# Turning the scaled keys on VectorE and through HBM, with the state's update one unit later, in a fused RWKV6 and SiLU kernel

## Chip, core and metric

The kernel runs on one core of one Trainium2 chip. The metric is the time of one execution on the device in microseconds (us): 628.24 us before the change, the median of three runs between 627.59 and 628.37. All tensors are fp32.

## What is computed

```python
# r, k, v, w: (4, 8, 768, 48), u: (8, 48)
for t in range(S):                                   # S = 768 tokens
    cur = einsum('bhd,bhe->bhde', u * k_t, v_t)
    y[:, :, t] = einsum('bhd,bhde->bhe', r_t, state + cur)
    state = w_t[:, :, :, None] * state + einsum('bhd,bhe->bhde', k_t, v_t)
x = y.transpose(0, 2, 1, 3).reshape(3072, 384)
h = x @ w_in                                         # 384 x 2048
out = (h / (1 + exp(-h))) @ w_out                    # 2048 x 384
```

The first half is a linear recurrence over tokens with a 48x48 state for each of 4 batches x 8 heads. The second half is a dense layer up, SiLU, and a dense layer down.

## The kernel before

**Units.** Tokens are cut into 6 chunks of 128, batches into 2 pairs. A unit is one chunk of one pair, so there are 12, numbered 0 to 11 here and in the code: the "fifth to tenth" units of the change are units 4 to 9. Units i and i + 2 are consecutive chunks of the same pair, so unit i + 2 is the next to read the state that unit i updates.

**Within a unit.** Keys are scaled by products of the decays w, queries likewise, in seven levels of doubling block size. Scores of a level are a small matmul (line 669), merged into the score tile by VectorE under a mask (`keep_masked`, line 679). When all levels are done, the tile `tk` holds keys scaled to the end of the chunk. Then `y_state` (line 794) multiplies queries by the old state, `y` (line 807) multiplies scores by values, and `update` (line 813) makes the new state: keys times values in PSUM tile `p_kv` (line 821), the old state decayed by GpSimd (line 826), their sum by VectorE (line 835).

**Turning the keys.** `tk` has the head dimension on partitions, and `update` wants tokens there. `turn_k` (line 773) turns it: eight TensorE transposes of 128x128 against an identity a unit (line 781), into PSUM, and two ScalarE copies to the tile `kq` (line 782).

**Turning the inputs.** `load_blocks` (line 100) loads w, r and k in 32-token blocks into `raw`, a buffer with two slots (unit i and unit i + 2 share one), in 16 small transfers for each of the three tensors and unit, all issued on SyncE's queue. `turn` (line 346) turns them on VectorE, two 32x32-block transposes for each tensor (line 360).

**The dense half** runs behind by one and two units. `up` (line 924) is 12 matmuls into one of two PSUM buffers `p_h` and one ScalarE SiLU out of it (line 938), so the third `up` can start only when the SiLU of the first has emptied its buffer. The down layer is done in seven block products, `quarter` (line 981), each 16 matmuls into one of two PSUM buffers `p_o` (line 995), emptied by ScalarE for the first (line 1002) and by VectorE for the rest (line 1004).

**Order.** The schedule is written out by hand: every engine does its instructions in the order in which the program lists them. `mix` (line 867) gives a unit as a list of groups. For units from 4 on there are eleven, 0 to 10; the main loop runs a group and then some steps of the dense half:

```python
room = (1, 1, 0, 2, 1, 1, 1, 1, 1, 2, 2, 1, 1, 0) if i < NPAIR else (3, 2, 2, 1, 1, 1, 2, 1, 1, 1, 0)
for group, count in zip(groups, room):
    do(*group)
    for step in steps[:count]:
        do(*step)
```

The steps are the seven quarters of unit i - 2 (after groups 0, 1 and 2) and the eight `up` of unit i - 1 (one after each of groups 3, 4 and 5, two after group 6, one after each of 7, 8 and 9). Group 3 holds the scores of levels 3 and 4 (`burst`), the move of the small block sums through HBM (`block_move`, line 537) and the large token loads of the next unit (`load_rk`, line 131). Group 5 prepares levels 5 and 6 (a ScalarE copy at line 595 and one at line 739). Group 6 spreads the block sums (ScalarE, lines 548 and 550; then VectorE, lines 551 and 557). Group 7 holds the scores of levels 5 and 6. Group 9 turns the keys and the next unit's inputs. Group 10 holds `y_state`, `y`, `update` and `move_x` (line 849), which brings y into the layout of the dense half in ten transfers.

**Loads.** The transfers of `load_blocks` for unit i + 2 are twelve list entries of four transfers each, w first, then k, then r, with `load_values` for unit i + 1 in the middle. They are spread over groups 1 to 10 (line 916), always at the end of a group, so ahead of the dense steps that follow the group.

Of the kernel before, what the change touches and what calls it, by code (L numbers as in the profile page):

```python
# [8 lines left out]
F32 = mybir.dt.float32  # L9
# [29 lines left out]
def kernel(  # L39
# [11 lines left out]
    nc = tc.nc  # L51
# [5 lines left out]
    NB = 2  # L57
    NP = H // 2
    PD = 64
    Q = NB * NP  # L60
# [5 lines left out]
    units = [(n, b0) for n in range(S // L) for b0 in range(0, B, NB)]  # L66
    NSLOT = 2
    NTOK = 2
    NPAIR = 4
# [4 lines left out]
    const = ctx.enter_context(tc.tile_pool(name="const", bufs=1))  # L74
    pin = ctx.enter_context(tc.tile_pool(name="pin", bufs=1))
    pt = ctx.enter_context(tc.tile_pool(name="pt", bufs=2))
# [4 lines left out]
    raw = const.tile([128, NSLOT, 3, NB, H, PD], F32, name="raw")  # L81
    WRK = {"w": 0, "r": 1, "k": 2}
# [17 lines left out]
    def load_blocks(i, name, g):  # L100


        n, b0 = units[i]
        src, t0 = {"w": w, "r": r, "k": k}[name], n * L + g * 32
        room = raw[:, i % NSLOT, WRK[name]].rearrange("p b h d -> p (b h d)").rearrange("p (q g d) -> p q g d", q=Q, d=32)
        for e in range(2):
            for a in range(2):
                d0, d1 = a * 32, min(D, a * 32 + 32)
                nc.sync.dma_start(out=room[(2 * e + a) * 32:(2 * e + a + 1) * 32, :, g, 0:d1 - d0],
                                  in_=src[b0:b0 + NB, e::2, t0:t0 + 32, d0:d1].rearrange("b q t d -> t (b q) d"))  # L110

    def load_values(i):
# [54 lines left out]
    scratch = ctx.enter_context(tc.tile_pool(name="scratch", bufs=2, space=bass.MemoryType.DRAM))  # L167
# [109 lines left out]
    room = pt.tile([128, 4, DM // 2], F32, name="partial", bufs=1).rearrange("p x d -> p (x d)")  # L277
# [66 lines left out]
    tw, tr, tk, diag, kq, xt = {}, {}, {}, {}, {}, {}  # L344
# [106 lines left out]
    at = 768  # L451
# [312 lines left out]
    def turn_apart(i):  # L764

        apart[i] = [ps.tile([128, NB, NP, D], F32, name="p_sc", bufs=2) for e in range(2)]
        for x in range(Q):
            for e, to in enumerate(apart[i]):
                rows = slice(PD * e, PD * e + D)
                nc.tensor.transpose(to[:, x // NP, x % NP], tk[i][rows, NP + (x if x < NP else NP + Q - 1 - x), :],  # L770
                                    ident[rows, rows])

    def turn_k(i, b):
        kq[i, b] = pt.tile([128, NP, 2 * PD], F32, name="kq")
        if i < NTOK:
            for e, have in enumerate(apart[i]):
                nc.scalar.copy(out=kq[i, b][:, :, PD * e:PD * e + D], in_=have[:, b])
            return
        p_tr = ps.tile([128, NP, 2 * PD], F32, name="p_m", bufs=2)
        for p in range(NP):  # L780
            nc.tensor.transpose(p_tr[:, p, :], tk[i][:, NP + (p, 2 * NP - 1 - p)[b], :], ident)  # L781
        nc.scalar.copy(out=kq[i, b], in_=p_tr)

    p_yt, p_kv, yt = {}, {}, {}

# [75 lines left out]
    def both(fn, i, *args):  # L861
        return [(fn, i, b, *args) for b in range(NB)]

    def block_loads(i):
        return [(load_blocks, i, name, g) for name in "wkr" for g in range(4)]

    def mix(i):

        ahead = i + 1 < len(units)

        def at(now, *steps):
            return steps if now else ()

        def bonus_steps(j, *steps):
            return [(block_bonus, j, x) for x in steps]

        def sum_steps(j, *steps):
            return [(block_sum, j, x) for x in steps]

        def turns(j):  # L880
            return [*both(turn, j, "w"), (product, j, 0), *both(turn, j, "k"), *both(turn, j, "r"), (grow_own, j, 0)]

        def start(j):
            return [*[(product, j, l) for l in range(1, NL)], (grow_own, j, 1)]

        end = [[*at(ahead, *bonus_steps(i + 1, 0, 1, 2, 3))],
               [*at(i < len(units) - NB, *both(turn_k, i)), *at(ahead, *turns(i + 1))],
               [*both(y_state, i), *both(y, i), *both(update, i), *at(ahead, *start(i + 1)),
                *at(ahead, *sum_steps(i + 1, 0, 1), *bonus_steps(i + 1, 4, 5)), (move_x, i)]]
        if i < NPAIR:  # L890
            groups = [[*both(turn, i, "w"), (product, i, 0)],
                      [*both(turn, i, "k"), *both(turn, i, "r"), (odd_ones, i)], [(start_levels, i), (prepare_keys, i, 1)],
                      [(prepare, i, 1), *[(product, i, l) for l in range(1, NL)]],
                      [(burst, i, 1), (keep_level, i, 1)],
                      [(keep_level, i, 2), (go_on, i, 2)],
                      [(prepare, i, 3), (reverse_v, i), (bonus, i, 0)],
                      [(burst, i, 3), (keep_level, i, 3), (bonus_sum, i, 0), (bonus, i, 1), (bonus, i, 2)],
                      [(keep_level, i, 4), (go_on, i, 4), (bonus_sum, i, 1), (load_rk, i + 1), (load_u,)],
                      [(prepare, i, 5), (make_block_mask,), (bonus_spread, i), (bonus_write, i)],
                      [(burst, i, 5), (keep_level, i, 5), (keep_level, i, 6), (go_on, i, 6)], *end]  # L900
        else:
            groups = [[], [(odd_keys, i, 2), (grow_keys, i, 2, False), (grow_queries, i, 2), *sum_steps(i, 2)],
                      [(prepare, i, 3), *bonus_steps(i, 6, 7)],
                      [(burst, i, 3), (keep_level, i, 3), *sum_steps(i, 3, 4), (block_move, i), *at(ahead, (load_rk, i + 1))],
                      [(keep_level, i, 4), (go_on, i, 4)],
                      [(prepare, i, 5), (reverse_v, i)],
                      [(block_spread, i), (block_write, i)],
                      [(burst, i, 5), (keep_level, i, 5), (keep_level, i, 6), (go_on, i, 6)], *end]

        loads = block_loads(i + NSLOT) if i + NSLOT < len(units) else []  # L910
        if i + 1 < len(units):
            loads.insert(len(loads) // 2, (load_values, i + 1))

        behind = groups[10 if i < NPAIR else 1:]
        for at, group in enumerate(behind):
            group += loads[at * len(loads) // len(behind):(at + 1) * len(loads) // len(behind)]
        return groups
# [114 lines left out]
    def back(fn, i, *args):  # L1032
# [6 lines left out]
       (make_dense,), (beat, 16))  # L1039

    blocks = block_loads(2)
    others = {1: [(clear, 0), (beat, 6)], 2: [(turn, 1, 0, "r"), (head_weight, 0), (beat, 2)],
              3: [(turn, 1, 1, "r"), (head_weight, 1), (beat, 2)], 4: [(turn, 1, 1, "w"), (reverse_v, 0)],
              5: [(bonus_spread, 0), (bonus_write, 0), (turn, 1, 0, "w")], 6: [*both(turn_in, 1, "k"), *blocks[0:4], (tail_weight, 0)]}
    for l in range(1, NL):
        do((scores, 0, l), *[(grow_keys, 0, l + 1)] * (l + 1 < NL), *others[l])

    do((bonus, 1, 0), (bonus, 1, 1), (bonus, 1, 2), *both(y, 0), (turn_apart, 0), (join_weight, 0), (add_weight,),
       (product, 1, 0), (tail_weight, 1), (turn, 1, 0, "k"), (join_weight, 1), (dense_x, 0, 0), (turn, 1, 1, "k"),
       (dense_x, 0, 1), (grow_queries, 1, 0), (odd_ones, 1), (tail_weight, 2), *both(turn_k, 0), (head_weight, 2),  # L1050
       (start_keys, 1, nc.gpsimd, True), (add_weight,), (up, 0, 0), (join_weight, 2), *blocks[4:8],
       (start_keys, 1, nc.gpsimd, False), (add_weight,), (tail_weight, 3), (odd_keys, 1, 1), (head_weight, 3), (grow_keys, 1, 1),
# [11 lines left out]
    for m in range(1, 4):  # L1064
# [3 lines left out]

    do((scores, 1, NL - 1), (join_weight, 8), (add_weight,), (up, 0, 7), *both(y, 1), (turn_apart, 1),
       (tail_weight, 9), *both(turn_k, 1), (dense_x, 1, 0), (head_weight, 9, [0]), (dense_x, 1, 1), (head_weight, 9, [1]),  # L1070
       (join_weight, 9), (add_weight,), (tail_weight, 10), (head_weight, 10), *both(update, 1), (up, 1, 0), *both(turn, 2, "w"))
    blocks = block_loads(3)

    others = {0: [(up, 1, 1), (down, 0, 0, 0), *both(turn, 2, "k"), (product, 2, 0), (product, 2, 1)],
# [20 lines left out]
    for i in range(3, len(units)):  # L1095
        steps = downs(i - 2) + ups(i - 1)
        groups = mix(i)
        if i == NTOK + 1:

            groups[2].append((weight_sums, 2))  # L1100
            groups[4].insert(1, (weight_sums, 3))
# [5 lines that stand above are left out]
            steps = steps[count:]  # L1107
# [32 lines left out]
```

## Time and profile before

| | |
|---|---|
| time, median of 3 | 628.24 us |
| span of the profiled execution | 626.6 us |
| TensorE matmul, share of span | 99% |
| VectorE | 70% |
| GpSimd | 58% |
| ScalarE | 30% |
| all transfers | 203067 packets, 53.25 MB, mean 85 GB/s |
| of these under 512 bytes | 186752 packets |

One unit in the middle of the kernel, from one burst of level 3 to the next, takes 48.74 or 48.75 us for units 4 to 9. Units 10 and 11 update no state and take 47.15 us.

How to read it: busy shares are averages over the whole span. The chain of waits is followed back from the last instruction to what released it; its shares say which engine and line the end hung on. A row of a timeline gives the start in us from the start of the span, how long it lasted, the engine (SPq is SyncE's queue), the line of the kernel, the tiles and the count; a bracket at its end is the idle time ahead of it and what ended that. A row of the groups ends with busy us and mean ns of one instruction, then the idle time ahead of them.

### The profile page before, as it was taken

The page shows a single profiled execution, that of the slowest core. Times are in us where ns is not written, and L with a number is a line of the kernel's source. Part 1 is how long each engine was busy: PE and PEld are TensorE (multiplying, and loading weights), DVE is VectorE, ACT ScalarE, POOL GpSimd, SP SyncE. Part 2 cuts the span into 40 slices and gives each one's busy share as a digit, 9 for nine tenths or more (in the row PEclk, how much of TensorE's full clock was granted, in tenths as well). Part 3 has the DMA queues.
Part 4 walks back from the last instruction along what each step waited for, and adds up shares of the span by engine and source line. Part 5 has one row for each costly group of instructions (what it writes and reads, how often), then busy time and mean ns, then how long its engine had stood idle before and what let it go on. Part 6 is the DMA issues. An engine that isn't in the chain of part 4 may idle for free.

```text
span 626.6 us, 12324 instructions
## 1 busy us (share of the span) xinstructions
PE 620.3 (99%) x4606; PEld 562.8 (90%) x4606; DVE 438.6 (70%) x749; ACT 187.4 (30%) x380; POOL 363.7 (58%) x414
## 2 busy tenths in 40 slices
PE   8999999999999999999999999999999999999997
PEld 8888876799899899899899899889889989989997
DVE  6879779898995694794794595686596596571041
ACT  6798882221321320320320321221221221220110
POOL 6998388566676567567577378378378458400000
PEclk9999999999999999999999999999999999999999
DMA  9966874443543643543543543542542312100000
GB/s 227 291 154 163 164 203 49 88 79 66 101 68 50 133 66 68 106 69 63 105 67 54 110 65 52 115 64 51 115 70 50 77 33 51 35 1 27 25 1 25
DMA packets 203067, 53.25 MB, mean 85 GB/s; under 512 B 186752, under 2 KB 194816, under 8 KB 203008
## 3 DMA queue, kind: packets, MB, share of 16 engines
q1 hardware_dynamic: 201424, 51.88, 41.1%
q10 hardware_dynamic: 1584, 0.59, 0.4%
q8 instruction: 36, 0.59, 0.4%
q14 instruction: 23, 0.19, 0.1%
HBM read 43.21 MB, written 5.24 MB: 77 GB/s over the span
## 4 chain that ended last, share of the span: by engine, by line
PE 94%; POOL 1%; DVE 1%; ACT 1%; DMA 1%; issue 1%; POOLq 0%; ACTq 0%
PE p_h L929 41%; PE p_o L995 32%; PE p_sc L669 5%; PE p_m L951 3%; PE p_m L807 3%; PE p_m L794 3%; PE p_m L669 3%; PE p_m L781 1%; PE p_sc L821 1%; DMA raw<-in_k_dram 1%; PE p_m L372 1%; POOL tk L625 1%; PE p_m L845 0%; DVE score L584 0%; POOL w_in_sb L241 0%
## 5 line engine op out<-in xcount | busy, mean ns | idle before, releaser
L929 PE MATMUL p_h<-xt,w_in_sb 128*128 128x256 f32 x1152 | 258.1, 382 | 0.7 <-POOL tk L649 0.7
L929 PEld LDWEIGHTS p_h<-xt,w_in_sb 128*128 128x128 f32 x1152 | 215.9, 190 | 32.6 <-POOL tk L649 0.9
L938 ACT ACTIVATE gt<-p_h 128x512 f32<-128x512 f32 x90 | 53.7, 597 | 256.1 <-PE p_h L929 255.9
L625 POOL TENSOR_TENSOR tk<-tk,tw 128x256 f32<-128x256 f32 x128 | 88.7, 714 | 62.4 <-ACT tk L595 34.7
L995 PE MATMUL p_o<-own,temps 128*128 128x192 f32 x528 | 87.9, 326 | 0.0
L995 PE MATMUL p_o<-w_out_sb,gt 128*128 128x192 f32 x508 | 87.3, 328 | 0.0
L995 PEld LDWEIGHTS p_o<-own,temps 128*128 128x128 f32 x528 | 86.0, 190 | 0.2
L995 PEld LDWEIGHTS p_o<-w_out_sb,gt 128*128 128x128 f32 x508 | 82.7, 190 | 0.9 <-issue 0.4
L487 POOL TENSOR_TENSOR ruk<-tokens_rk 128x768 f32<-128x768 f32 (+1 forms) x32 | 48.5, 1527 | 46.3 <-DMA tokens_rk<-in_k_dram 33.7
L977 DVE TENSOR_TENSOR temps<-gt 128x256 f32<-128x256 f32 x84 | 55.4, 660 | 18.3 <-ACT gt L938 18.3
L408 POOL TENSOR_TENSOR tw<-tw 128x256 f32<-128x256 f32 (+6 forms) x83 | 43.8, 528 | 40.2 <-DVE tw L360 36.3
L679 DVE COPY_PREDICATED score<-mask,p_sc 128x512 f32<-128x512 int8 x62 | 44.5, 772 | 13.4 <-PE p_sc L669 12.7
L607 DVE TENSOR_TENSOR tr<-tr,tw 128x512 f32<-128x512 f32 x61 | 49.6, 813 | 3.7 <-POOL tk L625 1.1
L595 ACT COPY tk<-tk 128x256 f32<-128x256 f32 x52 | 20.9, 403 | 85.4 <-POOL tk L625 67.1
L1004 DVE TENSOR_TENSOR partial<-p_o,partial 128x192 f32<-128x192 f32 x33 | 11.8, 358 | 47.2 <-PE p_o L995 47.1
L669 PEld LDWEIGHTS p_sc<-tr,tk 48*128 48x128 f32 x512 | 31.4, 187 | 10.3 <-issue 7.3
L669 PE MATMUL p_sc<-tr,tk 48*128 48x128 f32 x512 | 37.7, 285 | 0.7 <-POOL tk L625 0.6
L1004 DVE TENSOR_TENSOR temps<-p_o,partial 128x192 f32<-128x192 f32 x22 | 7.9, 358 | 33.3 <-PE p_o L995 23.1
L995 PE MATMUL p_o<-w_out_sb,temps 128*128 128x192 f32 x176 | 30.4, 326 | 0.0
L995 PEld LDWEIGHTS p_o<-w_out_sb,temps 128*128 128x128 f32 x176 | 28.9, 190 | 0.0
L487 POOL TENSOR_TENSOR tokens_rk<-tokens_rk,tokens_w 128x192 f32<-128x192 f32 (+1 forms) x32 | 26.8, 857 | 1.3
L977 DVE TENSOR_TENSOR temps<-temps,gt 128x256 f32<-128x256 f32 x43 | 25.7, 598 | 1.5
(170 smaller groups left out, 828.0 us busy)
## 6 DMA issues: line engine op xcount, KB each, us to landing
w_out_sb<-in_moe_w_in_dram SPq DMA_DIRECT2D x6, 768.0 KB, 7.0
w_out_sb<-in_moe_w_out_dram SPq DMA_DIRECT2D x4, 768.0 KB, 5.1
own<-in_moe_w_out_dram SPq DMA_DIRECT2D x4, 768.0 KB, 5.1
tokens_rk<-in_r_dram SPq DMA_DIRECT2D x8, 384.0 KB, 4.5
tokens_rk<-in_k_dram SPq DMA_DIRECT2D x8, 384.0 KB, 5.3
tokens_w<-in_w_dram SPq DMA_DIRECT2D x8, 384.0 KB, 6.6
xt<-yt SPq DMA_DIRECT2D x60, 48.0 KB, 2.0
raw<-in_w_dram SPq DMA_DIRECT2D x80, 32.0 KB, 2.3
```

The lines of the kernel that those rows point to most:

```text
L408: engine.tensor_tensor(out=up, in0=t[:, :, 0::2], in1=t[:, :, 1::2], op=ALU.mult)
L487: mul = lambda out, one, two: nc.gpsimd.tensor_tensor(out=out, in0=one, in1=two, op=ALU.mult)
L595: nc.scalar.copy(out=keys(i, X[(l + 1) % 2] * L + c, [4 * c, blocks], [c, 2], [1, c]), in_=keys(i, NP * L + c, [4 * c, blocks], [NP * L + ...
L607: nc.vector.tensor_tensor(out=odd, in0=odd, in1=tw[i][l][:, :, 0::2][:, :, :, None].to_broadcast([128, Q, L >> (l + 1), c]), op=ALU.mult)
L625: nc.gpsimd.tensor_tensor(out=out, in0=have, in1=odd_products(i, l, b, *blocks), op=ALU.mult)
L669: nc.tensor.matmul(bass.AP(tensor=s_p.tensor, offset=s_p.offset, ap=[s_p.ap[0], [apart * L // 2, 2], [1, L // 2]]), lhsT=tk[i][rows, X[l % ...
L679: nc.vector.copy_predicated(out=dst, mask=masks[l][:, :, None].to_broadcast([128, NB, NP, ni, c]), data=sc[e].rearrange("p (b q) (i c) -> ...
L929: nc.tensor.matmul(p_h[:, a, :], lhsT=w_in_sb[:, c, f * 128:(f + 1) * 128], rhs=xt[i][:, c, :], start=(c == 0), stop=(c == KC - 1))
L938: nc.scalar.activation(out=gt[i, m], in_=p_h, func=AF.Silu)
L977: nc.vector.tensor_tensor(out=out, in0=one, in1=two, op=op)
L995: nc.tensor.matmul(p, lhsT=left(f), rhs=right[:, f, :], start=(f == 0), stop=(f == FH - 1))
L1004: nc.vector.tensor_tensor(out=to, in0=p, in1=known, op=ALU.add)
```

## The change

For units 4 to 9 the keys are no longer turned on TensorE. VectorE turns the 32x32 blocks of `tk` into the room of the w slot in `raw` that it has just read (`turn_keys`), four transfers put the blocks in their places in a scratch tensor in HBM, and four more, early in the next unit, bring them into one tile for all keys (`load_keys`). That takes TensorE's transposes and ScalarE's copies away for these units. Since the keys come back only in the next unit, `update` of a unit runs in the next one, after its `y`; values are thus needed one unit longer, and the load of values, whose two buffers would otherwise be taken too early, moves to the start of their own unit. The block loads for units 6 to 11 come in the order k, r, w, since the w room is in use for longer, and those of r are issued on ScalarE's queue in place of SyncE's.

```diff
@@ load_blocks
-                nc.sync.dma_start(out=room[...], in_=src[...])
+                queue = nc.scalar if i > NPAIR + 1 and name == "r" else nc.sync
+                queue.dma_start(out=room[...], in_=src[...])
@@
+    all_keys = const.tile([128, Q, 2 * PD], F32, name="all_keys")
     def turn_k(i, b):
-        kq[i, b] = pt.tile([128, NP, 2 * PD], F32, name="kq")
+        kq[i, b] = all_keys[:, b * NP:(b + 1) * NP]
@@
+    def turn_keys(i):
+        room = raw[:, (i + 1) % NSLOT, WRK["w"]].rearrange("p b h d -> p (b h d)")
+        to = room.rearrange("p (g x d) -> p x g d", g=4, d=32)
+        for b in range(NB):
+            row0 = NP + b * NP
+            x = to[:, b * NP:(b + 1) * NP]
+            nc.vector.transpose(out=x[:, ::-1] if b == 1 else x, in_=tk[i][:, row0:row0 + NP, :].rearrange("p q (g d) -> p q g d", d=32))
+        turned_keys[i] = scratch.tile([32, Q * 4, 4, 32], F32, name="turned_keys")
+        for x in range(4):
+            nc.sync.dma_start(out=turned_keys[i][:, :, x], in_=room[x * 32:(x + 1) * 32].rearrange("t (y d) -> t y d", d=32))
+
+    def load_keys(i):
+        have = turned_keys.pop(i).rearrange("t (g q) x d -> t g q (x d)", g=4)
+        for b in range(NB):
+            kq[i, b] = all_keys[:, b * NP:(b + 1) * NP]
+        for g in range(4):
+            nc.sync.dma_start(out=all_keys[g * 32:(g + 1) * 32], in_=have[:, g])
@@ block_loads
-        return [(load_blocks, i, name, g) for name in "wkr" for g in range(4)]
+        return [(load_blocks, i, name, g) for name in ("wkr" if i < NPAIR + NSLOT else "krw") for g in range(4)]
@@ mix
-            return [*both(turn, j, "w"), (product, j, 0), ...]
+            return [*both(turn, j, "w"), *at(NPAIR <= j - 1 < len(units) - NB, (turn_keys, j - 1)), (product, j, 0), ...]
@@
+        ready = i if i < NPAIR else i - 1
-               [*at(i < len(units) - NB, *both(turn_k, i)), *at(ahead, *turns(i + 1))],
-               [*both(y_state, i), *both(y, i), *both(update, i), ...
+               [*at(i < NPAIR, *both(turn_k, i)), *at(ahead, *turns(i + 1))],
+               [*both(y_state, i), *both(y, i), *at(i != NPAIR and ready < len(units) - NB, *both(update, ready)), ...
@@
-            groups = [[], [(odd_keys, i, 2), ...
+            groups = [[*at(i > NPAIR, (load_values, i)), *at(NPAIR <= i - 1 < len(units) - NB, (load_keys, i - 1))], [(odd_keys, i, 2), ...
@@
-        if i + 1 < len(units):
+        if i < NPAIR:
             loads.insert(len(loads) // 2, (load_values, i + 1))
```

## The prediction

> **What bounds the kernel now.** I read the page's busy shares and chain of waits first, then a table of stretches by unit.
>
> ```profile
> PE 620.3 (99%) x4606; PEld 562.8 (90%) x4606; DVE 438.6 (70%) x749; ACT 187.4 (30%) x380; POOL 363.7 (58%) x414
> PE 94%; POOL 1%; DVE 1%; ACT 1%; DMA 1%; issue 1%; POOLq 0%; ACTq 0%
> 392.67:441.42 48.75, 48.75 (x363) 45.30 (x362) 34.40 (x60) 10.78 (x24) 30.88 (x35) 1.00 0.42 74
> 490.16:537.31 47.15, 47.15 (x323) 43.62 (x322) 33.83 (x58) 9.81 (x22) 29.15 (x33) 1.00 0.23 54
> ```
>
> TensorE is busy for the whole of a unit (first row of stretches: unit 8; columns: stretch, PE, PEld, DVE, ACT, POOL busy). A microsecond off its queue is a microsecond off the time, and one that it waits is added. Unit 10, without keys and update, is 1.60 us shorter. The operations concerned, by group:
>
> ```profile
> L781 PE MATMUL p_m<-ident,tk 128*128 128x128 f32 x64 | 8.3, 273 | 0.0
> L782 ACT COPY kq<-p_m 128x512 f32<-128x512 f32 x16 | 8.5, 588 | 0.0
> L360 DVE STREAM_TRANSPOSE tk<-raw 128x512 f32<-128x512 f32 x20 | 12.7, 671 | 0.0
> ```
>
> In the chain in order of time, the eight transposes of a unit take 0.87 us ("PE p_m L781 x8"), 0.109 each; 273 ns is the pipelined length. Now the timelines of unit 8 where ScalarE is to get transfers: ScalarE, then SyncE, then VectorE somewhat later, then the waits of SyncE's queue (total us, times, longest).
>
> ```profile
> 400.07 0.60 ACT L938 ACTIVATE gt<-p_h 128x512 f32<-128x512 f32 x1 [1.70 <-PE p_h L929]
> 400.86 0.62 ACT L739 COPY tr<-tr 128x512 f32<-128x512 f32 x1
> 402.66 0.60 ACT L938 ACTIVATE gt<-p_h 128x512 f32<-128x512 f32 x1 [1.18 <-PE p_h L929]
> 405.25 0.60 ACT L938 ACTIVATE gt<-p_h 128x512 f32<-128x512 f32 x1 [0.84 <-PE p_h L929]
> ```
> ```profile
> 401.88 0.59 SPq L139 DMA_DIRECT2D tokens_w<-in_w_dram  x1
> 402.52 5.89 SPq L109 DMA_DIRECT2D raw<-in_w_dram  x8
> 408.45 3.92 SPq L109 DMA_DIRECT2D raw<-in_k_dram  x8
> ```
> ```profile
> 428.93 0.36 DVE L1004 TENSOR_TENSOR temps<-p_o,partial 128x192 f32<-128x192 f32 x1
> 431.06 0.36 DVE L1004 TENSOR_TENSOR partial<-p_o,partial 128x192 f32<-128x192 f32 x1 [1.77 <-PE p_o L995]
> ```
> ```profile
> SPq L109 <- DMA tokens_w<-in_w_dram: 10.0, 7, 2.2
> ```
>
> Eight block loads take 3.92 us to issue (0.49 each), but 5.89 behind the token loads. The last row says why: a block load waits for a token load that shares no buffer with it. The trace's records of the 753 issues name the cause: completion is told on eight semaphores taken in strict turn, and an issue first waits for the transfer eight places earlier. The turn is common to both queues: SyncE's issue at 4.30 us waits for the semaphore that ScalarE's load of 0.74 us had signalled.
>
> [...]
>
> **The change, part by part**
>
> *Transposes off TensorE.* 6 units x 8 x 0.109 = 5.2 us, all on the path. The 12 ScalarE copies (588 ns) were off it: 0.
>
> *Transposes on VectorE.* Two a unit, 1.26 us a pair (the pair of line 360 at 417.14). Their keys are final at 402.3, the queue reaches them at about 417: no wait. Behind them stand the turns of k and r, the sums, the reductions, and then line 1004 for the second quarter; for that, TensorE waits at the fourth quarter. In unit 8 quarters start at 422.95 and take 18.40 / 7 = 2.63, so the fourth starts at 430.84, and line 1004 ended at 429.29: slack 1.55. TensorE comes 0.87 sooner and VectorE 1.26 later, 2.13 in all. Over units 4 to 9 the slack is 0.49, 1.73, 1.74, 1.56, 1.55 and 1.74 us, so TensorE waits 1.64 + 0.40 + 0.39 + 0.57 + 0.58 + 0.39 = 4.0 us. Of the 5.2 some 1.2 is left. [...]
>
> *Stores and loads of the keys.* Eight issues, about 0.49 each as the nearest row, 3.9 us a unit on SyncE, which loses 16 x 0.49 = 7.8: 0. The keys are wanted a whole unit after they are written.
>
> *Update one unit later, values in their own unit.* Same work. The decay (line 826) no longer waits for `y_state`. Value loads go out when SyncE is through with the previous unit, about 436.4 for unit 9, take 2.4 to issue, land some 2.8 later, near 442; VectorE wants them at 448.35: 0.
>
> *Loads of r on ScalarE.* By the list arithmetic, entries r0 and r1 (eight transfers) end group 5, r2 ends group 6, r3 group 7. So the eight stand between the copy of line 739 (dispatched at 400.86) and the SiLU at 402.66, the third `up`'s. That SiLU must end by 405.2, where the fourth `up` ended and the fifth wants its buffer: slack 1.9 us. Issuing alone takes 8 x 0.49 = 3.9.
>
> And they wait. The eight transfers ahead of them in the list are k2 and k3, which follow the token loads on SyncE as the eight w loads of 402.52 do now. These landed behind the tokens, at 408.35 (the first) to 409.83 (the last), the token load of w at 408.08. So ScalarE issues from 408.35 to 412.3, the SiLU ends at 412.9, and the fifth `up` starts at 412.95 instead of 405.2. For units 5 to 9 the token load of w landed 14.70, 14.45, 15.11, 15.41 and 15.37 us after the burst, mean 15.0; adding 0.27 + 3.92 + 0.60 + 0.08 and taking off 12.53, the fifth `up`'s old start, gives a wait of 7.3. Six units: 44 us. If the turn of semaphores puts w0 (the next entry on SyncE) between, the last wait ends near 411.9, and little changes. r2 and r3 wait for r0 and r1, long landed. [...]
>
> Sum: 628.2 - 5.2 + 44 + 2 = 669 us.
>
> **Rivals**
>
> 1. *Coupled queues*, as above: 669 us, with 655 to 680 for its terms. For it: the common turn of semaphores, and token loads that land 6 us after ScalarE wants to issue.
> 2. *Issue time alone.* If the program's turn of semaphores puts r0 and r1 ahead of the token loads, their waits are old. The third SiLU then ends 3.9 + 0.6 after 400.86 or 401.48, at 405.4 to 406.0: TensorE waits 0.35 to 0.95. [...] Less 0.87, a unit loses 0.1 to 2.4: 629 to 642, say 635. Against it: in the trace the token loads are issued by 402.5 and the next block loads follow at once.
> 3. *All hidden*, faster. ScalarE is busy 30%, and if issue costs it less than on SyncE, or the waits are elsewhere, the saving shows: 623.0 whole, 627.0 with the wait at the fourth quarter. For it: TensorE's 0.87 us a unit is certain. Against it: 3.9 us of issue in 1.9 of slack.
>
> **How the numbers follow.** Coupled queues 0.58, issue alone 0.17, hidden 0.25; nothing measured before shows two queues at work in a unit, which is why the last keeps a quarter. The likeliest gives 669. The range runs from 623, the whole saving, to 680, token loads landing 2 us later in each unit. Faster by over 0.2% (under 627.0) is most of the third case, 0.24; within 0.2% the rest of it and the low end of the second, 0.08; slower 0.68.
>
> **What would show it.** Right: TensorE idle about 7 us in units 4 to 9 ahead of the fifth `up`, put down to line 938; ScalarE idle ahead of its issues at line 109, for a transfer; unit length 55 us instead of 48.75. The second case shows no such wait, but eight issues of 0.49 us and stops under 1 us. The fourth quarter's stop shows as TensorE waiting for line 1004. Wrong: units of 47.9 us with TensorE without gaps, or line 781 gone with no wait at ScalarE's issues.

## The result and the profile after

The changed kernel takes 680.18 us (median of 6 runs, 678.48 to 683.31), the kernel before 627.98 us on the same chip. The ratio is 1.0836, with an interval of 1.0810 to 1.0863: 52.2 us slower. That is past the upper end of the forecast range (680 us) by 0.2 us, and 11 us above the predicted 669.

The page after, busy shares and chain of waits, then two rows of the table of stretches: unit 8 and unit 10 (columns as before: stretch and its length, PE, PEld, DVE, ACT, POOL busy, TensorE's granted clock, DMA share, GB/s).

```profile
PE 625.6 (92%) x4558; PEld 563.5 (83%) x4558; DVE 453.1 (67%) x761; ACT 181.6 (27%) x368; POOL 362.6 (53%) x414
PE 59%; DVE 21%; DMA 6%; issue 5%; SPq 3%; ACT 2%; ACTq 2%; POOL 2%; DVEq 0%; POOLq 0%
425.34:483.36 58.02, 49.68 (x355) 45.54 (x354) 37.51 (x62) 9.81 (x22) 30.97 (x35) 0.94 0.44 82
541.09:588.96 47.87, 47.87 (x353) 44.48 (x352) 35.27 (x60) 9.80 (x22) 31.43 (x35) 1.00 0.23 54
```

TensorE carried 94% of the chain before and carries 59% now; VectorE has 21%, transfers and the two issuing queues 11%. Unit 8 has grown from 48.75 to 58.02 us, with TensorE idle for 8.3 us of it and its clock at 0.94. From unit 4 to unit 9 the units last 50.82, 58.78, 58.73, 59.38, 58.02 and 57.83 us. Unit 10 has no stop. It is 0.72 us longer than before, because it now does the update of unit 9.

Where does TensorE stop? Its timeline in unit 8 (the burst of level 3 began at 425.34):

```profile
441.40 1.06 PE L670 MATMUL p_m<-tr,tk 48*128 48x128 f32 x16
448.35 9.51 PE L955 MATMUL p_h<-xt,w_in_sb 128*128 128x256 f32 x36 [5.89 <-ACT gt L964]
...
472.70 5.47 PE L1021 MATMUL p_o<-own,temps 128*128 128x192 f32 x32 [2.45 <-DVE temps L1030]
```

There are two stops. The first, 5.89 us, is ahead of the *sixth* `up`, behind the burst of level 5 (its matmuls are the first row), and waits for ScalarE's SiLU. The second, 2.45 us, is ahead of the fourth quarter and waits for VectorE. The five `up` ahead of the burst of level 5 run without a gap in unit 8. Over units 4 to 9 the first stop takes 1.17, 6.75, 6.09, 7.29, 5.89 and 5.74 us, 32.9 in all, and the second 12.5.

Now SyncE's timeline in the same unit, then ScalarE's (ACTq is its queue of issues), then rows of the waits of SyncE's queue and of the waits of all engines (us in total, times, longest).

```profile
421.77 1.35 SPq L807 DMA_DIRECT2D all_keys<-turned_keys  x3
434.63 3.94 SPq L110 DMA_DIRECT2D raw<-in_k_dram  x8
...
439.63 0.41 SPq L541 DMA_DIRECT2D kept<-block_sums  x1
441.36 1.00 SPq L544 DMA_DIRECT2D spare<-kept  x2
442.45 1.24 SPq L140 DMA_DIRECT2D tokens_rk<-in_r_dram  x1
```
```profile
430.15 0.60 ACT L964 ACTIVATE gt<-p_h 128x512 f32<-128x512 f32 x1 [9.29 <-PE p_h L955]
432.74 0.60 ACT L964 ACTIVATE gt<-p_h 128x512 f32<-128x512 f32 x1 [1.70 <-PE p_h L955]
432.85 0.82 ACTq L110 DMA_DIRECT2D raw<-in_r_dram  x2
...
433.71 2.97 ACTq L110 DMA_DIRECT2D raw<-in_r_dram  x6
436.73 0.60 ACT L964 ACTIVATE gt<-p_h 128x512 f32<-128x512 f32 x1 [2.58 <-DMA raw<-in_r_dram]
444.44 0.24 ACT L549 COPY spare<-spare 128x64 f32<-128x64 f32 x1 [7.11 <-DMA spare<-kept]
...
447.70 1.08 ACT L964 ACTIVATE gt<-p_h 128x512 f32<-128x512 f32 x2 [2.01 <-DMA tokens_rk<-in_r_dram]
```
```profile
SPq L110 <- DMA raw<-in_r_dram: 59.3, 21, 11.8
```
```profile
ACT spare L549 <- DMA spare<-kept: 36.8, 6, 8.1
```

SyncE is ready for its k loads at 423.1, when the loads of the keys are issued, and issues the first at 434.63: 11.5 us of nothing. It waits for the first load of r, which ScalarE could issue only at 432.85, behind its SiLU, and which landed at 434.57. The semaphores in the trace's records of these issues show why. The eight take turns in the order 100, 102, 103, 104, 105, 106, 108, 110: in the kernel before, each of the 753 issues has the next one of this order. The four loads of the keys have 106, 108, 100 and 104, the first eight loads of r 110, 102, 103, 105, 106, 108, 100 and 103, and the first load of k has 110 again. So the first load of r stands between the second and the third load of the keys in the turn, and the first load of k eight places behind it. Behind the k loads stand the move of the block sums (`kept`, `spare`), 14.3 us after the burst instead of 4.2 before, and the token loads. So ScalarE's copy at line 549 waits for the block sums, the SiLUs of the fourth and fifth `up` stand behind it, and the sixth `up` has no free buffer. The last 2.01 us ahead of these SiLUs are an issue of r that waits for a load of tokens, which is itself late on SyncE's queue.

For comparison, the move in unit 8 of the kernel before, and VectorE's merge of the block sums there (that unit's burst began at 392.60):

```profile
396.83 0.33 SPq L540 DMA_DIRECT2D kept<-block_sums  x1
404.71 2.50 DVE L557 COPY_PREDICATED score<-spare 128x1024 f32<-128x1024 int8 x2
```

The chain of waits in order of time, followed back from TensorE's restart at 472.70 (start, us, piece), says it in one piece:

```profile
434.72 0.46 ACTq L110
435.22 2.04 DMA raw<-in_r_dram
437.27 0.31 SPq L110
...
439.63 1.71 DMA kept<-block_sums
441.36 3.06 DMA spare<-kept
444.44 0.24 ACT spare L549
...
445.99 1.35 DVE score L558 x2
...
451.46 1.96 DVE temps L1003
...
472.28 0.37 DVE temps L1030
...
472.70 2.38 PE p_o L1021 x13
```

A load of r on ScalarE's queue, a load of k on SyncE's that has nothing to do with it, the block sums, ScalarE's spread, and then 27 us of VectorE's queue without a break to the second quarter's addition. Ahead of these rows the chain runs through TensorE's burst and first two `up`, to 432.76; from there to the fourth quarter TensorE is not in it.

The lengths of the units fit this chain. In units 5 to 9 the block sums are moved 15.3, 15.6, 16.2, 14.4 and 14.4 us after the burst, 10.2 to 12.0 us later than before. VectorE's merges (line 558), which need them, begin 21.2, 21.4, 22.1, 20.7 and 20.3 us after the burst instead of 12.1, so they are late by 9.1, 9.3, 10.0, 8.6 and 8.2 us; some 2 us of the delay are slack that the sums had. With the loads of r on SyncE (the first experiment below), a unit whose block sums are in time takes 49.18 us. The five units here are longer than that by 9.6, 9.6, 10.2, 8.8 and 8.7 us, within 0.5 us of the lateness of their merges.

### The profile page after: what moved, and what is told of

It reads as the page before. It is cut to its first block, busy times and chain, and to the rows that moved or that the text cites. A ratio compares the mean times of both kernels' runs of the same rounds, so it can differ in the third digit from the quotient of the medians.

```text
span 678.3 us, 12232 instructions
## 1 busy us (share of the span) xinstructions
PE 625.6 (92%) x4558; PEld 563.5 (83%) x4558; DVE 453.1 (67%) x761; ACT 181.6 (27%) x368; POOL 362.6 (53%) x414
## 4 chain that ended last, share of the span: by engine, by line
PE 59%; DVE 21%; DMA 6%; issue 5%; SPq 3%; ACT 2%; ACTq 2%; POOL 2%; DVEq 0%; POOLq 0%
PE p_h L955 24%; PE p_o L1021 23%; DVE temps L1003 9%; PE p_sc L670 4%; PE p_m L977 3%; DMA raw<-in_r_dram 3%; DVE tr L608 3%; DMA spare<-kept 2%; PE p_m L670 2%; ACTq L110 2%; SPq L110 2%; PE p_m L832 1%; DMA kept<-block_sums 1%; DVE score L558 1%; DVE score L680 1%
## 5 line engine op out<-in xcount | busy, mean ns | idle before, releaser
L955 PE MATMUL p_h<-xt,w_in_sb 128*128 128x256 f32 x1152 | 266.5, 391 | 33.9 <-ACT gt L964 33.2
L955 PEld LDWEIGHTS p_h<-xt,w_in_sb 128*128 128x128 f32 x1152 | 222.8, 196 | 69.5 <-ACT gt L964 35.1
L626 POOL TENSOR_TENSOR tk<-tk,tw 128x256 f32<-128x256 f32 x128 | 88.7, 713 | 52.3 <-ACT tk L596 34.7
L1021 PE MATMUL p_o<-own,temps 128*128 128x192 f32 x528 | 89.5, 328 | 12.5 <-DVE temps L1030 12.5
L1021 PEld LDWEIGHTS p_o<-own,temps 128*128 128x128 f32 x528 | 85.9, 190 | 14.4 <-DVE temps L1030 14.2
L1003 DVE TENSOR_TENSOR temps<-gt 128x256 f32<-128x256 f32 x84 | 63.4, 754 | 18.3 <-ACT gt L964 18.3
L608 DVE TENSOR_TENSOR tr<-tr,tw 128x512 f32<-128x512 f32 x61 | 51.6, 847 | 3.7 <-POOL tk L626 1.1
L635 POOL TENSOR_TENSOR tk<-tk,tw 128x256 f32<-128x256 f32 x32 | 27.3, 871 | 7.1 <-DVE tk L361 7.1
```

What stands on the lines that cost most here:

```text
L608: nc.vector.tensor_tensor(out=odd, in0=odd, in1=tw[i][l][:, :, 0::2][:, :, :, None].to_broadcast([128, Q, L >> (l + 1), c]), op=ALU.mult)
L626: nc.gpsimd.tensor_tensor(out=out, in0=have, in1=odd_products(i, l, b, *blocks), op=ALU.mult)
L635: nc.gpsimd.tensor_tensor(out=have, in0=have, in1=odd_products(i, l, b, [2, NP * ni]), op=ALU.mult)
L955: nc.tensor.matmul(p_h[:, a, :], lhsT=w_in_sb[:, c, f * 128:(f + 1) * 128], rhs=xt[i][:, c, :], start=(c == 0), stop=(c == KC - 1))
L1003: nc.vector.tensor_tensor(out=out, in0=one, in1=two, op=op)
L1021: nc.tensor.matmul(p, lhsT=left(f), rhs=right[:, f, :], start=(f == 0), stop=(f == FH - 1))
```

## Experiments

Theory: the common turn of completion semaphores makes SyncE wait for transfers that ScalarE issues late. Rivals: SyncE has too many issues, whoever loads r; ScalarE's time of issue; VectorE's longer queue; the half clock behind the stops. Times of before in the four series were 628.42, 628.2, 628.3 and 628.2 us.

### The loads of r back on SyncE

```diff
-                queue = nc.scalar if i > NPAIR + 1 and name == "r" else nc.sync
+                queue = nc.sync
```

> The changed kernel with one part undone: the loads of r go back to SyncE's queue, in the order k, r, w. Theory (SyncE is held by the common turn of the eight completion semaphores until ScalarE issues r, so the block sums come late and ScalarE's SiLUs behind them too): without a second queue nothing holds SyncE, the stops of TensorE ahead of the sixth up and the slow clock after them go, and 627 to 635 us are left (5.2 us saved, 4 to 12 us of waiting at the fourth quarter). Rival (SyncE has too little issue time for the new transfers, so r had to move): over 640 us, with value or block loads late.

Measured: 632.38 us, ratio 1.0068 (1.0051 to 1.0085). 47.8 of the 52.2 us are gone, no stop is left ahead of an `up`, and the profiled execution has a mean clock of 0.999. So the route of the keys through HBM, the late update and the late values cost little; the queue for r, in the order k, r, w, costs nearly all. But the kernel is still not faster than before. What is left is ahead of the fourth quarter, some 1.0 us a unit (3.16 in unit 5). TensorE's row in unit 8, then VectorE's timeline, then GpSimd's decay of the state; last, the product of line 608 (line 607 there) and the decay in the kernel before:

```profile
433.67 2.54 PE L1021 MATMUL p_o<-own,temps 128*128 128x192 f32 x14 [1.05 <-DVE temps L1030]
```
```profile
419.80 1.30 DVE L796 STREAM_TRANSPOSE raw<-tk 128x512 f32<-128x512 f32 x2
...
423.66 1.54 DVE L608 TENSOR_TENSOR tr<-tr,tw 128x512 f32<-128x512 f32 x1
...
433.26 0.36 DVE L1030 TENSOR_TENSOR temps<-p_o,partial 128x192 f32<-128x192 f32 x1
```
```profile
423.60 2.50 POOL L851 TENSOR_TENSOR state<-state,tw 128x512 f32<-128x512 f32 x2
```
```profile
419.62 0.88 DVE L607 TENSOR_TENSOR tr<-tr,tw 128x512 f32<-128x512 f32 x1
419.91 2.66 POOL L826 TENSOR_TENSOR state<-state,tw 128x512 f32<-128x512 f32 x2
```

VectorE never pauses from the sums to the addition of line 1030, which comes 38.2 us after the burst; before it came 36.3 us after it. Of these 1.9 us the transposes are 1.34. The product of line 608 is 0.66 more (1.54, against 0.88 before). It stands beside GpSimd's decay of the state in both kernels; but before it began 0.29 us ahead of the decay, and now it begins 0.06 us behind it. The first of the decay's two instructions changes the other way, from 1.49 to 1.04 us. In unit 4 of this run, which decays no state, the product takes 1.10 us. So in these traces whichever of the two began first was the shorter for it; no run tested that alone. The other rows together shift by 0.1 to 0.2 us the other way.

### The queue alone, on the kernel before

```diff
-                nc.sync.dma_start(out=room[...], in_=src[...])
+                queue = nc.scalar if i > NPAIR + 1 and name == "r" else nc.sync
+                queue.dma_start(out=room[...], in_=src[...])
@@ block_loads
-        ... for name in "wkr" ...
+        ... for name in ("wkr" if i < NPAIR + NSLOT else "krw") ...
```

> The kernel before with nothing but the load change: order k, r, w and r on ScalarE's queue for units 6 to 11. Theory (the second queue is what costs): clearly slower, 637 to 660 us, with TensorE waiting for ScalarE's SiLU, although no key is turned on VectorE. Rival (the turning of keys and its transfers cost the time): within 1% of 628 us.

Measured: 646.23 us, 1.0289 (1.0265 to 1.0312): the queue, with the order k, r, w that goes with it, costs 18 us without any of the rest. Here, in units 5 to 9, the wait is the one that the prediction described. TensorE, then ScalarE, in unit 8:

```profile
421.73 2.64 PE L930 MATMUL p_h<-xt,w_in_sb 128*128 128x256 f32 x11 [2.40 <-ACT gt L939]
```
```profile
414.97 0.62 ACT L740 COPY tr<-tr 128x512 f32<-128x512 f32 x1
419.11 1.92 ACTq L110 DMA_DIRECT2D raw<-in_r_dram  x2
421.08 0.60 ACT L939 ACTIVATE gt<-p_h 128x512 f32<-128x512 f32 x1 [5.49 <-DMA tokens_rk<-in_k_dram]
```

The issue at 419.11 waits for a load of tokens on SyncE, the third SiLU is held, and the *fifth* `up` stops for 1.6 to 2.4 us. The block sums move at 4.2 us. In unit 4 it is the other way round, as in the changed kernel: the move comes at 11.3 us and the unit takes 56.4 us. In this run the two queues thus wait for each other in both directions, ScalarE for 5.49 us in unit 8 and SyncE, with the move 7.1 us late, in unit 4. That the place of the loads of r in the turn decides which one waits is the author's reading.

### The loads of r first

```diff
-        ... else "krw") ...
+        ... else "rkw") ...
```

> The changed kernel with r first in the list (r, k, w), still on ScalarE's queue: r then ends groups 1 to 4, where ScalarE is mostly idle, and stands ahead of the block sums. Theory (the place of r in the list holds SyncE and the SiLUs, not the queue as such): 624 to 635 us, no stop ahead of the sixth up. Rival (eight issues of 0.49 us on ScalarE cost wherever they are): 640 us or more.

Measured: 694.1 us, 1.1037 (1.1016 to 1.1058). A miss: earlier loads of r were to free SyncE and held it up more. The first row of the waits of SyncE's queue:

```profile
SPq L110 <- DMA raw<-in_r_dram: 86.4, 16, 9.2
```

The loads of r now stand ahead of `move_x` and of the values as well, and ScalarE comes to them no sooner than its compute lets it. Here it is a copy, ahead of unit 8, that waits for GpSimd:

```profile
428.20 0.40 ACT L596 COPY tk<-tk 128x256 f32<-128x256 f32 x1 [7.74 <-POOL tk L626]
428.29 0.32 ACTq L110 DMA_DIRECT2D raw<-in_r_dram  x1
```

In the chain `move_x` follows a load of r that landed at 432.2, then come the block loads and the values, and the block sums move at 449.5, 14.3 us after the burst. TensorE now also stops early in a unit, up to 1.7 us at once, where matmuls of `up` wait for the transfers of `move_x`. What counted in these runs was not where the loads are in the list, but how late ScalarE issued them compared with what SyncE had next in the turn.

### Block loads from the fourth group on

```diff
-        behind = groups[10 if i < NPAIR else 1:]
+        behind = groups[10 if i < NPAIR else 3:]
```

> The changed kernel with the twelve load entries spread over groups 3 to 10 in place of 1 to 10, so that no block load stands ahead of the move of the block sums in SyncE's queue; r stays on ScalarE. Theory (the late block sums are the link between the queues and TensorE's stop): the move is issued some 4 us after the burst again in place of 14 to 16, and the time falls to 626 to 645 us. Rival (ScalarE's own waits for transfers make the stop): still over 660 us.

Measured: 633.15 us, 1.0074 (1.0046 to 1.0102). With r still on ScalarE, but with the block sums and tokens ahead of every block load, SyncE moves the sums 4.2 us after the burst in each unit, and units 5 to 9 take 49.0 to 49.2 us (in the profiled execution of 630.9 us). The late block sums are the link. ScalarE still waits for 48.1 us at SiLUs behind its issues, and little of it reaches TensorE:

```profile
ACT gt L964 <- DMA raw<-in_r_dram: 48.1, 13, 6.5
PE p_h L955 <- ACT gt L964: 4.5, 6, 1.8
```

### The order k, w, r, and nothing else

```diff
-        ... else "krw") ...
+        ... else "kwr") ...
```

> The changed kernel with one word altered: the block loads in the order k, w, r instead of k, r, w, still from the second group of steps and with r on ScalarE, and the state's update as in the change. Theory (the whole loss beyond 1% is where the loads of r stand in ScalarE's program and in the turn of semaphores): SyncE moves the block sums 4.2 to 5 us after the burst, no stop ahead of the sixth up, stops of about 1.05 us ahead of the fourth quarter in six units as with the loads on SyncE (632.4 us), 628 to 632 us. Rival (any load of r on ScalarE holds SyncE up while block loads go out from the second group): the move at 10 us or later and over 650 us.

Measured: 629.76 us, 1.0026 (1.0016 to 1.0037). One word of the change takes away 50 of the 52 us. Sixteen loads of r are still on ScalarE, but later, eight of them behind the last SiLUs:

```profile
412.65 1.82 ACTq L110 DMA_DIRECT2D raw<-in_r_dram  x4
415.23 0.60 ACT L964 ACTIVATE gt<-p_h 128x512 f32<-128x512 f32 x1 [1.99 <-DMA raw<-in_r_dram]
415.24 1.82 ACTq L110 DMA_DIRECT2D raw<-in_r_dram  x4
...
421.51 5.93 ACTq L110 DMA_DIRECT2D raw<-in_r_dram  x8
427.48 0.32 ACT L1028 COPY partial<-p_o 128x192 f32<-128x192 f32 x1 [5.39 <-DMA raw<-in_r_dram]
```

SyncE still waits for loads of r (30.5 us in all ahead of block loads, 17.0 ahead of the stores of keys), but later in the unit, where nothing urgent is behind them: the block sums move at 4.2 us in units 5 to 9. The stops that remain are ahead of the fourth quarter, 0.5 to 1.04 us in units 4 to 9, where VectorE still carries the transposes; unit 8 has another of 0.28 us ahead of the third quarter, which waits for ScalarE's copy of line 1028, the last row above.

### A filled stop

In units 5 to 9 of the changed kernel TensorE gets half its clock for 6.83 us from within each long stop, 3.0 to 4.9 us of it behind the stop's end. Is that a cost of its own?

```diff
-                      [(burst, i, 5), (keep_level, i, 5), ...
+                      [(burst, i, 5), *at(NPAIR < i < len(units) - NB, (fill, 48)), (keep_level, i, 5), ...
+    def fill(n):
+        p = second[0].tile([128, L], F32, name="p_o", bufs=2)
+        for x in range(n):
+            nc.tensor.transpose(p, ident, ident)
```

> The changed kernel as it is, with 48 transposes of the identity on TensorE (48 x 0.109 = 5.2 us) put between the burst of level 5 and the sixth up of units 5 to 9, where TensorE stops for 5.7 to 7.3 us; nothing reads what they write. Theory (the half clock that follows the stop costs some 9.5 us of the 680.2): the clock stays whole, the stop is shorter by what fills it, 669 to 673 us. Rival (the slower matmuls behind the stop are hidden by other waits, or the clock does not follow the stop): 678 to 683 us.

Measured: 691.88 us, 1.1038 (1.1007 to 1.1068), outside both expectations. TensorE in unit 8 (from 434.6 on), then two stretches of it:

```profile
457.99 8.04 PE L955 MATMUL p_h<-xt,w_in_sb 128*128 128x256 f32 x36 [0.79 <-ACT gt L964]
...
482.30 2.93 PE L1021 MATMUL p_o<-own,temps 128*128 128x192 f32 x8 [3.75 <-DVE temps L1030]
```
```profile
478.50:485.30 6.80, 3.04 (x10) 3.00 (x10) 5.68 (x13) 0.40 (x1) 4.63 (x7) 0.71 0.32 60
485.30:488.00 2.70, 2.70 (x10) 2.70 (x10) 0.17 (x1) 0.45 (x2) 2.62 (x5) 0.50 0.30 46
```

Filled, the first stop leaves the clock whole: 36 matmuls take 8.04 us instead of 9.51. But the fourth quarter starts no earlier, 47.7 us after the burst in unit 8 (47.4 without the filling), and 48.2, 48.3, 48.5 and 48.8 us in units 5, 6, 7 and 9 (48.2, 48.1, 48.8, 47.2). So the half clock behind the sixth `up`'s stop was beside VectorE's chain and cost nothing. TensorE comes to the fourth quarter sooner, waits 3.75 us there, and has the half clock *behind* that stop, where its own queue sets the time: 5.0 to 5.8 of the 6.83 us, so 2.5 to 2.9 us a unit, where the units are 2.2 to 4.0 us longer. The profiled execution took 696.62 us at a mean clock of 0.973; four of the six took 691.15 to 692.45 us at 0.98, so with less half clock. By these timelines a half clock cost time only behind the last wait of the unit.

### The transposes on VectorE left out

The loads of r on SyncE, and

```diff
-            nc.vector.transpose(out=x[:, ::-1] if b == 1 else x, in_=tk[i][...])
```

> The changed kernel with the loads of r on SyncE, and without the two VectorE transposes of the scaled keys; the stores and loads through HBM stay. Left out is the turn of the keys, so the state of the fifth to tenth unit is updated with other values; all other work is there. Theory (the transposes' 1.26 us in VectorE's queue are the whole cost of the route through HBM): no stop ahead of the fourth quarter, units 47.9 us, 623.5 to 626.5 us, against 632.4 with them. Rival (stores, loads or the late update cost something themselves): 628 to 632 us.

Measured: 627.12 us, 0.9986 (0.9976 to 0.9996), between the two expectations. Against the ratio of 1.0068 with the transposes that is 5 us. In the profile (of an execution of 625.48 us) units 7 and 8 take 47.87 us without a stop, just what the saving on TensorE promised. In units 5, 6 and 9 stops of 0.5 to 0.9 us remain. There SyncE moved the block sums 6.2 to 7.2 us after the burst, and VectorE's merges of line 558 began 13.1, 13.7 and 13.0 us after it, against 12.1 in units 7, 8 and 10. So the transposes on VectorE are the larger part of what is left when r is loaded by SyncE, and a SyncE that is late is the other.

### The state's additions behind the third quarter

The loads of r on SyncE, and the two additions of line 860 as a step of their own, one unit on:

```diff
     def update(i, b):
-        if b < NB - 1:
-            return
+        if b == NB - 1 and i < NPAIR:
+            add_state(i)
+    def add_state(i):
         for e in range(2):
@@ groups of mix
-            ... [(odd_keys, i, 2), ...
+            ... [*at(NPAIR <= i - 2 < len(units) - NB, (add_state, i - 2)), (odd_keys, i, 2), ...
```

> The changed kernel with the loads of r back on SyncE, and the two VectorE additions that end the state's update (0.54 + 0.56 us) moved out of the update into the next unit, behind the third quarter's addition. With the loads on SyncE alone the time was 632.4 us, with a stop of 1.05 us a unit ahead of the fourth quarter. Theory (the stop is nothing but VectorE's queue ahead of the second quarter's addition, made longer by the 1.26 us of transposes): 1.1 us less in that queue takes the stop away, units 47.9 to 48.2 us, 624 to 627 us in all. Rival (VectorE as a whole, not one place in its queue, is what is short): the stop moves on to the next addition behind the moved ones, units stay at 49 us, 630 to 633 us.

Measured: 629.51 us, 1.0026 (1.0011 to 1.0040): 2.6 us better than without the late additions, by the two ratios, and short of the theory. Where SyncE is in time (units 7 to 9) the stop fell from 1.05 to 0.15, 0.32 and 0.37 us. In units 4, 5 and 6 the sums moved 7.1, 7.1 and 5.3 us after the burst, and 0.85 to 1.94 us remain. ScalarE's timeline in unit 6:

```profile
307.79 1.00 ACT L551 COPY spare<-spare 32x64 f32<-32x64 f32 x4 [1.53 <-DMA spare<-kept]
```

The block sums land late, the spread ends 1.5 us later, and VectorE begins its merges 13.0 and 13.6 us after the burst in units 5 and 6, 12.1 in 7 to 9. It is the changed kernel's chain once more, with 1 to 1.5 us in place of 11, from SyncE's own backlog: here eight k loads are issued ahead of the move.

### The same, with the block loads from the fourth group

Once with r on ScalarE:

> The changed kernel with the loads of r on ScalarE as they are, all block loads handed out from the fourth group of steps instead of the second, and the two additions of the state's update moved behind the third quarter's addition. With the loads from the fourth group alone the time was 633.2 us, units 49.0 us, with stops of 0.2 to 1.0 us ahead of the sixth up and 0 to 0.6 ahead of the fourth quarter. Theory (ScalarE's issues still cost the sixth up, the additions free only the fourth quarter): the stops ahead of the sixth up stay, 629 to 632 us. Rival (both stops come from the same long VectorE queue): 624 to 627 us.

Measured: 630.01 us, 1.0027 (1.0016 to 1.0039), as the theory had it. The sums move at 4.2 us, no stop is left ahead of the fourth quarter, and 0.5 to 2.1 us a unit stay ahead of the sixth `up`, behind ScalarE's issues.

Once with r on SyncE:

> The changed kernel with the loads of r back on SyncE, all block loads handed out from the fourth group of steps, and the two additions of the state's update behind the third quarter's addition. With the same additions and the loads from the second group the time was 629.5 us: SyncE issued the block sums' move 7.1, 7.1 and 5.3 us after the burst in units 4 to 6, instead of 4.2, and the stops ahead of the fourth quarter were 0.85, 1.70 and 1.94 us there, but 0.15 to 0.37 in units 7 to 9. Theory (SyncE being late is what is left of the loss): the move at 4.2 us in all units, stops of 0 to 0.4 us, units 47.9 to 48.3 us, 623.5 to 626.5 us. Rival (the stops of units 4 to 6 have another cause): 628 to 631 us.

Measured: 631.21 us, 1.0039 (1.0025 to 1.0053): a miss. The move was at 4.2 us in unit 4, but at 4.5 to 6.5 in units 5 to 10. In units 5, 6 and 9 VectorE's merges begin 13.2, 13.5 and 13.0 us after the burst, and the stops are 1.55, 1.79 and 2.13 us; in 7 and 8 they begin at 12.1, and the stops are 0.47 and 0.66. With all 48 block loads of a unit pushed into its later groups, the end of the list is still on SyncE's queue when the next unit's values, keys and block sums are due.

### The order k, w, r, from the fourth group, with the late additions

```diff
-        ... else "krw") ...
+        ... else "kwr") ...
-        behind = groups[10 if i < NPAIR else 1:]
+        behind = groups[10 if i < NPAIR else 3:]
```

> The changed kernel with the loads of r on ScalarE, all block loads from the fourth group, in the order k, w, r, and the late additions: the sixteen loads of r so stand in the last three groups, away from the SiLUs of the fourth to sixth up. With the order k, r, w the time was 630.0 us and stops of 0.5 to 1.2 us stood ahead of the sixth up. Theory (the stops ahead of the sixth up are ScalarE's time of issue before it, so they go where the issues go): none ahead of the sixth up, 624 to 627 us; a stop elsewhere would be ahead of the first up of the next burst or at the copies of y. Rival (the turn of semaphores again ties SyncE's next transfers to ScalarE's late ones, as with the order r, k, w): over 632 us.

Measured: 626.8 us, 0.9974 (0.9965 to 0.9982), so 1.5 us less than before and 53 less than the change. No stop is left ahead of an `up`; the fourth quarter still stops for 0.3 to 1.2 us in units 6, 7 and 9. The idea of the change does pay, with 1.5 of the 5.2 us that TensorE saves, when the loads of r are where ScalarE has time and SyncE nothing urgent, and with the late additions.

## Why the prediction was wrong, step by step

The direction was right, and so was the cause at large: two queues tied by one turn of completion semaphores. The sum was wrong in three steps and right in the rest.

- **Transposes off TensorE, 5.2 us.** Right. Unit 10 after the change and the two free units without the transposes take 47.87 us: 48.74 less 0.87.
- **Loads of r on ScalarE, "the eight transfers ahead of them in the list are k2 and k3".** This is the step that failed. The prediction took the turn of the semaphores from the order of the list. In the built program the first loads of r stand among the loads of the keys in the turn, eight places ahead of the first loads of k; why it is built so, the runs do not show. So ScalarE's first loads of r don't wait for SyncE: SyncE waits for ScalarE, which comes to its issues behind the second SiLU, 7.5 us after the burst. SyncE stands still for 11.5 us in unit 8, and the block sums leave 10.2 to 12.0 us late in units 5 to 9. Of the prediction's picture, the stop ahead of the fifth `up` did not show; it is ahead of the sixth. "ScalarE idle ahead of its issues" for the token loads did show, but only for later issues: SiLUs waited for it six times, 13.2 us in all and at most 2.5 us at once. The kernel before with the queue alone has the forecast wait in five units, with stops of 1.6 to 2.4 us, not 7.3. That 44 and 32.9 us for the stop at an `up` are near each other is chance.
- **The case where the turn puts r ahead.** The second rival named it and looked only at ScalarE: "their waits are old", 635 us. It didn't ask who comes after r in the turn. On SyncE that was everything, the block sums among it.
- **Stores and loads of the keys, "SyncE, which loses 16 x 0.49 = 7.8: 0".** Taking issues off SyncE did not help a queue that then stood still for 11.5 us. And with all issues on SyncE the queue is not free of cost either: where its backlog delays the block sums enough, the merges begin 0.9 to 1.6 us late and the fourth quarter pays (3.16 us in unit 5 with r on SyncE, where they began at 13.6 us).
- **The fourth quarter, 4.0 us in the parts and 2 in the sum.** Too small: 12.5 us, 1.32 to 2.45 in each of units 4 to 9. No run shows the 2 us that the sum takes off, nor the late VectorE that is part of the second rival's 0.1 to 2.4 us a unit; these stops are what the changed kernel showed in their place. Part of the 12.5 is the chain above, since VectorE starts its merges late. With the coupling out of the way it is still 8.3. Steady units have 1.05 where 0.57 was forecast. The transposes have the forecast size (0.69 each, 1.3 a pair). By the timelines the missing term is the product of line 608, 0.66 us longer with r on SyncE, where it begins 0.06 us behind GpSimd's decay; no run tested it alone.
- **VectorE beside GpSimd's products (line 488, line 487 in the kernel before).** The token loads were taken to land as before; behind the late block sums they land near 448 in unit 8, and GpSimd's products, from 448.99 to 455.43 us, run beside VectorE's sums of line 1003, which take 2.03, 1.11 and 1.23 us where the next five take 0.41 or 0.42.
- **The clock** was in no step. The half clock of 6.83 us per long stop slows the `up` behind it (9.51 us for 36 matmuls instead of 8.04), but by the filled stop it lies beside VectorE's chain and adds nothing in the profiled execution.
- **Update and values later: 0.** About right: they are in the version that runs in 626.8 us. No run tests them alone.

Put right, the sum needs one large term. Late block sums lengthen units 5 to 9 by 46.8 us over five units of 49.18. That a unit with the sums in time takes 49.18 and not 47.87, VectorE's transposes and its product of line 608, is 6.6 us. Unit 4 is 3.7 longer than a unit without keys' turn and update (47.15). Less 5.2 for the transposes off TensorE, that is 51.9 us; measured were 52.2. That the range was missed by only 0.2 us owes something to two errors, the stop at the `up` too large and the rest too small.

## What to carry to other kernels

Here two queues shared one turn of eight completion semaphores, and each issue on the second, busy engine was a promise to the first queue: in unit 8 the transfer eight places later, and all that stood behind it on SyncE's queue, waited for 11.5 us until ScalarE got to its load of r and the data landed. Before moving transfers to another engine, find in the built program what stands behind them in the turn, and put them where the new issuer is through with its urgent work and the old queue has nothing urgent next; the one word for the order was worth 50 us here, while well-placed loads on ScalarE gained 2.6 us over leaving them on SyncE (629.8 against 632.4 us), and no run had the order k, w, r with the loads on SyncE, so the order may have part in this too. And when TensorE stops in several places, follow one chain to the last stop of the unit before summing the stops, because the earlier ones, and a half clock behind them, may lie beside it, as in unit 8, where the fourth quarter started 47.4 us after the burst with the first stop and 47.7 with the stop filled.

## What the runs showed of the hardware

- In the changed kernel the half clock comes in five stretches of 6.83 us, each with the longer stop of a unit. They begin at 270.46, 328.49, 386.51, 444.54 and 502.57 us, 58.03 us apart, which is 17 times 3.413, half a stretch. Laid on this grid from 190 us on, 16 pieces of 3.413 us at the whole clock that hold up to 1.80 us of stops (counting stops over 0.15 us) were followed by the whole clock, and five with 2.09 to 3.41 us by the half. The four stops of 2.14 to 2.45 us ahead of the fourth quarter fell into two pieces each, with at most 1.69 us in one, and were followed by none. Across kernels the length of a stop alone does not decide: the version with late additions, whose longest stop ahead of the fourth quarter is 1.94 us, has a mean clock of 0.997 in its profiled execution of 629.7 us, so 3 to 4 us at the half, and the one with the loads of r on SyncE, with a stop of 3.16 us, has 0.999, so less than 2 us.
- A stop ahead of the fourth quarter, where the unit has no other and no half clock, cost some 0.26 us more than its gap in the trace: with r on SyncE, a unit with a stop of 1.05 us lasts 49.18 us, 1.31 longer than one without (47.87). Why, no run shows.
- ScalarE's eight issues from 432.85 to 436.68 ran beside its copies of lines 596 and 740 and took 0.32 to 0.46 us each, as SyncE's eight beside and behind them did (0.31 to 0.45); what they held up was the next instruction that stood behind them, here the SiLU at 436.73, by 2.58 us.
